# Moving the angles, magnitudes and folds that prepare batch 1 inside tile 0 of a Fourier-mixing and SwiGLU kernel

## The chip, the cores and the metric

The kernel runs on one core of one Trainium2 chip. The metric is the device time of one execution in microseconds (us), lower is better. Before the change it was 700.46 us, the median of three runs (700.24 to 701.84). The record marks a run as slow when it is over 1.5% above the fastest of its kernel.

## The reference

```python
def _attn_ref(x):                         # x: 8 x 3008 x 256, float32
    X = np.fft.fft(x, axis=1)
    X = np.fft.fft(X, axis=2)
    return X.real.astype(np.float32)

def _moe_ref(x, w_gate, w_val, w_out):    # x: 24064 x 256, d_ff = 1536
    g = x @ w_gate
    silu = g * (1.0 / (1.0 + np.exp(-g)))
    val = x @ w_val
    return (silu * val @ w_out).astype(np.float32)

# reference: _moe_ref of _attn_ref(x), reshaped to 24064 x 256
```

## The kernel before

The kernel folds each batch of x by its symmetries, does the long Fourier transform as matmuls against tables of cosines and sines, puts the short transform into the SwiGLU weights, and then works through tiles of about 512 columns. A tile has 12 *units*, one for each 128 of the 1536 features. A unit has a first half (`part_a`: gate and value of output row k, their product into `hp`) and a second half (`part_b`: the mirrored row, into `hm`), and the second half is issued one unit later. From tile 2 on, about half of the units are *split*: there GpSimd and not VectorE makes the two products.

The code below is in the order in which it is issued; the engines run it in parallel, each in its own order.

```python
# tmp_ctx: memory of the start, given back before the tiles; its space is used again (sg, hp, ...)
mm_, mM = col("mm", 4), col("mM", 4)      # small columns in tmp_ctx; mM = m / M
...
def angles(rr, kf, ch, t1):               # VectorE; reads mM
    for i in range(2):
        vstt(rr[:, i, :], kf, mM[:, 2 * ch + i:2 * ch + i + 1], t1[:, i, :],
             op0=Alu.mult, op1=Alu.subtract)

def magnitude(ra, rr):                    # VectorE: clears the sign bit
    vts(ra.bitcast(I32), rr.bitcast(I32), scalar1=0x7FFFFFFF, scalar2=None, op0=Alu.bitwise_and)

def sine(ch, lo, hi, rr):                 # ScalarE
    nc.scalar.activation(Tab[:, ch, :, 1, lo:hi], rr, AF.Sin, scale=sc, bias=zero)

def cosine(ch, lo, hi, ra):               # ScalarE, of the magnitude
    nc.scalar.activation(Tab[:, ch, :, 0, lo:hi], ra, AF.Sin, scale=-sc, bias=halfpi)
...
transform(0, 0, (1,), acc)                # end of the start
value_rows((0,))
for ch in range(2):
    angles(rrO[:, ch], kfO, ch, rrO[:, ch].bitcast(I32))
tmp_ctx.close()
...
# folds of batch b: kind "C" reads XC, kind "A" reads XA; all write SDf, on GpSimd
spread(("C", 1), 14, 1, 12)               # 14 steps over units 1 to 12
spread(("A", 1), 14, 13, 24)
...
def cosines(ch):
    magnitude(rrO[:, ch], rrO[:, ch])     # in place: the sine must have read it
    cosine(ch, NOO, NTAB, rrO[:, ch])

before = {1: weight_unit(1, 0), 2: weight_unit(1, 1),      # ahead of unit i
          3: [lambda: sine(0, NOO, NTAB, rrO[:, 0])],
          4: weight_unit(2, 0),
          5: [lambda: sine(1, NOO, NTAB, rrO[:, 1])],
          6: weight_unit(2, 1) + [lambda: cosines(0)],
          7: [lambda: cosines(1)],
          8: [lambda: weigh(NOO, NTAB)],
          9: [lambda: value_rows((1, 2))]}
...
for i, u in enumerate(units):
    for fn in before.pop(i, ()): fn()
    if i == 10:
        loads[0:0] = ((("A", 1), fn) for fn in load_a(1, nc.sync))   # x of batch 1
    run_loads(3)                          # three waiting loads a unit
    part_a(u)
    ...                                   # part_b of the unit before, output matmuls
    for what, j in fold_at.get(i, ()):
        fold_step(what, j, i)             # step 0 first issues all loads that it needs
```

The tables of 4i+1 (the cosines and sines of output rows 1, 5, 9 and so on) are needed by the second transform of batch 0, at the end of unit 9.

Of the kernel before, what the change touches and what calls it, by code (L numbers as in the profile page):

```python
# [12 lines left out]
F32 = mybir.dt.float32  # L13
I32 = mybir.dt.int32
# [17 lines left out]
def kernel(  # L32
# [11 lines left out]
    P = 128  # L44
    H = M // 2
    G = M // 8
# [15 lines left out]
    NOO = NCE + GH + 1  # L62
    NTAB = NOO + G
# [10 lines left out]
    const = ctx.enter_context(tc.tile_pool(name="const", bufs=1))  # L74
# [17 lines left out]
    CD = const.tile([P, 2, P], BF16, name="CD")  # L92
    SDt = const.tile([P, 2, P], BF16, name="SDt")
    m2 = const.tile([P, 1], F32, name="m2")
    wC = const.tile([P, 1], F32, name="wC")
    sgn = const.tile([P, 1], F32, name="sgn")
    XA = const.tile([P, 8, 2, D], F32, name="XA")
    XC = const.tile([P, 8, 2, D], F32, name="XC")
    SDf = const.tile([P, 2, 4, D], F32, name="SDf")
# [6 lines left out]
    rrO = XA.rearrange("p a q d -> p (a q d)")[:, 4 * T:4 * T + 4 * G].rearrange("p (c q n) -> p c q n", c=2, q=2)  # L106
    kfO = XA.rearrange("p a q d -> p (a q d)")[:, 4 * T + 4 * G:4 * T + 5 * G]
# [109 lines left out]
    q = nc.sync  # L217
# [48 lines left out]
    def col(name, n=1, dt=F32):  # L266
        small[name] = tp.tile([P, n], dt, name=name)
        return small[name]


    mm_, mM = col("mm", 4), col("mM", 4)

    def m_cols(ch, p, L, j0):
        h = col(f"h{ch}", 1, I32)
# [28 lines left out]
    def angles(rr, kf, ch, t1):  # L303
# [4 lines that stand above are left out]
    def magnitude(ra, rr):  # L308
        vts(ra.bitcast(I32), rr.bitcast(I32), scalar1=0x7FFFFFFF, scalar2=None, op0=Alu.bitwise_and)

    def sine(ch, lo, hi, rr):
        nc.scalar.activation(Tab[:, ch, :, 1, lo:hi], rr, AF.Sin, scale=sc, bias=zero)

    def cosine(ch, lo, hi, ra):
        nc.scalar.activation(Tab[:, ch, :, 0, lo:hi], ra, AF.Sin, scale=-sc, bias=halfpi)

    def weigh(lo, hi):
        vts(Tab[:, 1, 1, :, lo:hi], Tab[:, 1, 1, :, lo:hi], scalar1=wC, scalar2=None, op0=Alu.mult)
# [123 lines left out]
    def value_rows(fcs):  # L442

        n = T // P
        ps = psO.tile([P, T], F32, name="o")
        for fc in fcs:
            src = W0[1] if fc == 0 else Wraw[1][:, :, (fc - 1) * T:fc * T]
            for f in range(n):
                for no in range(2):
                    nc.tensor.matmul(ps[:, fc * n + f:fc * n + f + 1], src[:, no, f * P:(f + 1) * P],  # L450
                                     SDt[:, no, 0:1], start=(no == 0), stop=(no == 1))
        nc.scalar.copy(w0[:, fcs[0] * n:(fcs[-1] + 1) * n], ps[:, fcs[0] * n:(fcs[-1] + 1) * n])
# [154 lines left out]
    unfolded(1, 1, SBc, False, True)  # L607
    transform(0, 0, (1,), acc)
    value_rows((0,))
    for ch in range(2):  # L610
        angles(rrO[:, ch], kfO, ch, rrO[:, ch].bitcast(I32))

    tmp_ctx.close()

# [156 lines left out]
    def spread(what, n, lo, hi):  # L771
        seq.extend((lo + (i * (hi - lo)) // (n - 1), what, i) for i in range(n))

    spread(("C", 1), 14, 1, 12)
    spread(("A", 1), 14, 13, 24)
    lo = 25
    for b in range(2, B, 2):
        u = slot[(b, 0)] - 1
# [48 lines left out]
    def weights(fc, gv, k):  # L827
        transform_w(fc, gv, k, psO.tile([P, T], F32, name="o"))()

    def cosines(ch):  # L830
        magnitude(rrO[:, ch], rrO[:, ch])
        cosine(ch, NOO, NTAB, rrO[:, ch])

    def weight_unit(fc, gv):
        return [lambda k=k: weights(fc, gv, k) for k in range(2)]

    before = {1: weight_unit(1, 0), 2: weight_unit(1, 1),
              3: [lambda: sine(0, NOO, NTAB, rrO[:, 0])],
              4: weight_unit(2, 0),
              5: [lambda: sine(1, NOO, NTAB, rrO[:, 1])],  # L840
              6: weight_unit(2, 1) + [lambda: cosines(0)],
              7: [lambda: cosines(1)],
              8: [lambda: weigh(NOO, NTAB)],
              9: [lambda: value_rows((1, 2))]}
    loads = []

    prev = None
# [67 lines left out]
```

## Time and profile before

| what | before |
|---|---|
| median of the runs | 700.46 us |
| TensorE busy, share of the span | 97% |
| unit 0's first matmul, unit 10's first matmul | 25.87 us, 57.21 us |
| mean granted clock, 25 to 58 us | 0.79 |
| first matmul of unit 33's transform | 111.01 us |

First come three lines of the profile's page. The first gives each engine's busy time, share of the span and instructions; the others cut the span into 40 slices of 17.5 us, with busy tenths for PE (TensorE) and the clock that TensorE was granted, in tenths.

```profile
PE 679.1 (97%) x4369; PEld 415.5 (59%) x4369; DVE 519.6 (74%) x925; ACT 433.9 (62%) x765; POOL 593.8 (85%) x577
...
PE   7879989999999999999999999999999999999997
...
PEclk9979999999999999999999999999999999999999
```

After the seventh slice TensorE is as good as full and its clock is whole. Time can only be won before that. Of the slices after the start, the third (35 to 52 us) has a busy digit of 7 and a clock digit of 7, and the sixth (about 87 to 105 us) a busy digit of 8.

Next are lines of TensorE's timeline in tile 0. The columns are start and duration in us, engine, source line, operation, output and input; the brackets give the idle time before the instruction and what ended it.

```profile
30.90 0.36 PE L754 MATMUL g<-Qt,Wm 128*128 128x480 bf16 x1 [1.68 <-ACT sg L744]
31.59 0.36 PE L754 MATMUL v<-Qt,Wm 128*128 128x480 bf16 x1 [0.33 <-DVE hp L745]
...
42.24 0.37 PE L717 MATMUL g<-Pt,Wp 128*128 128x480 bf16 x1
42.44 0.37 PE L717 MATMUL g<-Qt,Wq 128*128 128x480 bf16 x1
...
42.85 0.37 PE L717 MATMUL v<-Qt,Wq 128*128 128x480 bf16 x1
46.16 0.56 PE L754 MATMUL g<-Qt,Wm 128*128 128x480 bf16 x1 [2.95 <-ACT sg L744]
...
47.20 0.61 PE L717 MATMUL g<-Pt,Wp 128*128 128x480 bf16 x1
47.60 0.61 PE L717 MATMUL g<-Qt,Wq 128*128 128x480 bf16 x1
```

There are two idle times. TensorE waits 1.68 us and then 0.33 us in unit 1 (at 30.90 and 31.59), and 2.95 us in unit 7. After the second one, matmuls of 480 columns start 0.40 us apart (47.20, 47.60), where before it they started 0.20 us apart (42.24, 42.44). The clock record has TensorE at half clock from 31.9 to 35.3 us and from 45.5 to 55.7 us.

The causes stand in the timelines of VectorE (DVE), ScalarE (ACT) and GpSimd (POOL).

```profile
27.12 3.00 DVE L305 SCALAR_TENSOR_TENSOR XA<-XA,mM 128x376 f32<-128x376 f32 x4
30.88 0.66 DVE L745 TENSOR_TENSOR hp<-sg,v 128x480 bf16<-128x480 f32 x1 [0.76 <-ACT sg L744]
...
42.56 2.14 DVE L309 TENSOR_SCALAR XA<-XA 128x752 int32<-128x752 int32 x1
...
47.28 0.75 DVE L309 TENSOR_SCALAR XA<-XA 128x752 int32<-128x752 int32 x1
```

```profile
30.28 0.57 ACT L744 ACTIVATE sg<-g 128x480 f32<-128x480 f32 x1 [4.07 <-DMA XC<-in_x_dram]
...
44.73 0.92 ACT L315 ACTIVATE Tab<-XA,halfpi 128x752 bf16<-128x752 f32 x1 [2.92 <-DVE XA L309]
```

```profile
39.62 4.67 POOL L152 TENSOR_TENSOR SDf<-XC 64x1024 f32<-64x1024 f32 x2
...
46.93 0.69 POOL L437 TENSOR_SCALAR Wm<-Wq,m_89 128x512 bf16<-128x512 bf16 x1
...
50.40 0.69 POOL L437 TENSOR_SCALAR Wm<-Wq,m_89 128x512 bf16<-128x512 bf16 x1
...
69.78 4.67 POOL L152 TENSOR_TENSOR SDf<-XA 128x1024 f32<-128x1024 f32 x2 [6.13 <-DMA XC<-in_x_dram]
...
90.10 1.28 POOL L737 TENSOR_TENSOR hp<-sgv,vv 128x512 bf16<-128x512 f32 x1
...
95.39 2.35 POOL L152 TENSOR_TENSOR SDf<-XC 128x1024 f32<-128x1024 f32 x1 [1.32 <-DMA XA<-in_x_dram]
```

The four angle operations fill VectorE from 27.12 to 30.12, and the first Silu of unit 0 (`sg`, ScalarE) starts at 30.28 although its input was ready near 27. The profile names a load as what ended the 4.07 us of idle; the semaphores that this instruction waits for in the built program include VectorE's last angle operation, because `sg` lies in the memory that the start's small columns give back. In unit 7 the first cosine waits 2.92 us for a magnitude that took 2.14 us, while GpSimd was in its two 64x1024 folds (39.62 to 44.29).

GpSimd's first value product (`hp`) runs at 90.10, among the last steps of batch 1's second folds, which began at 69.78 after 6.13 us of waiting for x.

### The profile page before, as it was taken

To read this page: it belongs to the slowest core of one execution; us is meant where nothing else is said; L and a number is where in the kernel's file an instruction comes from. 1 tells how busy PE (TensorE), PEld (TensorE's weight loads), DVE (VectorE), ACT (ScalarE), POOL (GpSimd) and SP (SyncE) were. 2 spreads that over 40 slices of the span, in tenths; PEclk is the share of its full clock that TensorE was granted. 3 is DMA by queue.
4 is the path that set the end of the run, shared out by engine and by line. 5 is a ranking of instruction groups with operands and counts; after the bars stand their busy time and mean duration, and the time that the engine had idled before them with its cause. 6 is when DMAs were issued, how large, how long until landed. Compare 5 with 4: busy or idle time off the path is not lost.

```text
span 698.6 us, 13274 instructions
## 1 busy us (share of the span) xinstructions
PE 679.1 (97%) x4369; PEld 415.5 (59%) x4369; DVE 519.6 (74%) x925; ACT 433.9 (62%) x765; POOL 593.8 (85%) x577
## 2 busy tenths in 40 slices
PE   7879989999999999999999999999999999999997
PEld 4335655566565566565665656655666556656676
DVE  8776667777777778677777777777777777788862
ACT  7465655566565666565665666656666566656663
POOL 7896999899999999999998989998899655658930
PEclk9979999999999999999999999999999999999999
DMA  9636353241612412316125111117111011111112
GB/s 216 112 46 132 107 136 93 63 121 44 160 32 65 132 46 71 111 46 160 34 65 138 39 34 43 46 38 152 37 47 46 31 31 46 45 31 46 46 46 69
DMA packets 45567, 52.55 MB, mean 75 GB/s; under 512 B 6290, under 2 KB 33466, under 8 KB 45498
## 3 DMA queue, kind: packets, MB, share of 16 engines
q1 hardware_dynamic: 42314, 49.35, 26.0%
q0 software_dynamic: 3184, 2.36, 2.5%
q8 instruction: 34, 0.56, 0.3%
q14 instruction: 35, 0.29, 0.1%
HBM read 29.39 MB, written 24.65 MB: 77 GB/s over the span
## 4 chain that ended last, share of the span: by engine, by line
PE 83%; DMA 4%; DVE 4%; issue 4%; POOL 2%; ACT 1%; SPq 1%; ACTq 0%; POOLq 0%; DVEq 0%
PE o L677 32%; PE v L717 16%; PE g L717 15%; PE g L754 8%; PE v L754 4%; PE g L566 3%; PE v L566 3%; DVE vv L736 2%; DMA XC<-in_x_dram 2%; DMA XC_107<-in_x_dram 1%; DMA XA<-in_x_dram 1%; POOL hm L759 1%; DVE vv L734 1%; POOL hp L737 1%; PE g L854 1%
## 5 line engine op out<-in xcount | busy, mean ns | idle before, releaser
L737 POOL TENSOR_TENSOR hp<-sgv,vv 128x512 bf16<-128x512 f32 (+1 forms) x132 | 168.2, 1276 | 49.9 <-DVE vv L734 39.0
L759 POOL TENSOR_TENSOR hm<-sgv,vv 128x512 bf16<-128x512 f32 (+1 forms) x132 | 167.7, 1275 | 8.5 <-ACT sgv L758 8.1
L677 PE MATMUL o<-Wo,hm 128*128 128x256 bf16 (+2 forms) x1140 | 170.5, 273 | 0.0
L677 PE MATMUL o<-Wo,hp 128*128 128x256 bf16 (+2 forms) x1140 | 169.6, 273 | 0.0
L677 PEld LDWEIGHTS <-hp 128*128 128x128 bf16 (+2 forms) x1140 | 111.9, 98 | 68.1 <-issue 8.2
L677 PEld LDWEIGHTS <-hm 128*128 128x128 bf16 (+2 forms) x1140 | 112.2, 99 | 65.8 <-issue 6.6
L732 DVE SCALAR_TENSOR_TENSOR es<-bc,w_85,v 128x512 f32<-128x512 f32 (+1 forms) x132 | 98.1, 743 | 53.0 <-PE v L717 52.8
L745 DVE TENSOR_TENSOR hp<-sg,v 128x512 bf16<-128x512 f32 (+2 forms) x156 | 103.7, 665 | 36.7 <-ACT sg L744 35.9
L744 ACT ACTIVATE sg<-g 128x512 f32<-128x512 f32 (+2 forms) x156 | 90.8, 582 | 45.9 <-PE g L717 41.0
L762 ACT ACTIVATE sg<-g 128x512 f32<-128x512 f32 (+2 forms) x156 | 91.1, 584 | 44.4 <-PE g L754 44.2
L763 DVE TENSOR_TENSOR hm<-sg,v 128x512 bf16<-128x512 f32 (+2 forms) x156 | 103.2, 661 | 19.0 <-ACT sg L762 8.9
L754 PE MATMUL g<-Qt,Wm 128*128 128x512 bf16 (+2 forms) x288 | 108.8, 378 | 5.2 <-ACT sg L744 5.1
L717 PE MATMUL v<-Pt,Wp 128*128 128x512 bf16 (+2 forms) x288 | 108.6, 377 | 2.4 <-DVE vv L736 2.4
L758 ACT ACTIVATE sgv<-g 128x512 f32<-128x512 f32 (+1 forms) x132 | 78.9, 598 | 50.1 <-PE g L754 41.3
L717 PE MATMUL g<-Qt,Wq 128*128 128x512 bf16 (+2 forms) x288 | 108.6, 377 | 0.5 <-DVE Qt L579 0.5
L717 PE MATMUL g<-Pt,Wp 128*128 128x512 bf16 (+2 forms) x288 | 108.8, 378 | 0.1
L729 ACT ACTIVATE sgv<-g 128x512 f32<-128x512 f32 (+1 forms) x132 | 78.7, 596 | 45.0 <-PE g L717 35.9
L734 DVE SCALAR_TENSOR_TENSOR vv<-v,es 128x512 f32<-128x512 f32 (+1 forms) x132 | 91.1, 690 | 19.7 <-POOL hp L737 1.7
L736 DVE SCALAR_TENSOR_TENSOR vv<-v,es 128x512 f32<-128x512 f32 (+1 forms) x132 | 89.7, 680 | 6.2 <-POOL hm L759 3.3
L717 PEld LDWEIGHTS <-Wp 128*128 128x128 bf16 x576 | 56.6, 98 | 42.1 <-issue 5.8
L152 POOL TENSOR_TENSOR SDf<-XA 128x1024 f32<-128x1024 f32 x28 | 66.1, 2365 | 8.0 <-DMA XC<-in_x_dram 6.1
L683 ACT COPY ev<-o 128x512 f32<-128x512 f32 x90 | 52.8, 587 | 30.6 <-PE o L677 29.6
(173 smaller groups left out, 742.2 us busy)
## 6 DMA issues: line engine op xcount, KB each, us to landing
out_dram<-ev SPq DMA_DIRECT2D x96, 128.0 KB
XA<-in_x_dram SPq DMA_DIRECT2D x32, 256.0 KB
XA<-in_x_dram SPq DMA_DIRECT2D x112, 64.0 KB
XC<-in_x_dram SPq DMA_DIRECT2D x105, 32.0 KB
XC<-in_x_dram SPq DMA_DIRECT2D x28, 120.0 KB
out_dram<-ev SPq DMA_DIRECT2D x12, 120.0 KB
out_dram<-ev SPq DMA_DIRECT2D x10, 112.0 KB
XA<-in_x_dram SPq DMA_DIRECT2D x1, 1024.0 KB
```

What stands on the lines that cost most here:

```text
L677: nc.tensor.matmul(ps[:n, j, :], hts[minus][:, f, c:c + n], Wo[:, f, :], start=(f == 0), stop=(f == nF - 1))
L717: nc.tensor.matmul(ps[:, :w], Wt[:, gv, fs], src[:, :w], start=start, stop=stop, skip_group_check=True)
L732: stt(es[:, :w], bc[t][:, :w], w0[:, f:f + 1], e[:, :w], op0=Alu.mult, op1=Alu.add)
L734: stt(vp[:, :w], o[:, :w], -0.5, es[:, :w], op0=Alu.mult, op1=Alu.add)
L736: stt(vm[:, w - 1::-1], o[:, :w], 0.5, es[:, :w], op0=Alu.mult, op1=Alu.add)
L737: nc.gpsimd.tensor_tensor(hts[t][0][:, f, :w], sg[:, :w], vp[:, :w], op=Alu.mult)
L744: nc.scalar.activation(sg[:, :w], g[:, :w], AF.Silu)
L745: nc.vector.tensor_tensor(hts[t][0][:, f, :w], sg[:, :w], v[:, :w], op=Alu.mult)
L754: nc.tensor.matmul(ps[:, :w], Wm[:, gv, f * P:(f + 1) * P], Qt[:, :w], start=False, stop=True, skip_group_check=True)
L759: nc.gpsimd.tensor_tensor(hts[t][1][:, f, :w], sg[:, :w], v[:, :w], op=Alu.mult)
L762: nc.scalar.activation(sg[:, :w], g[:, :w], AF.Silu)
L763: nc.vector.tensor_tensor(hts[t][1][:, f, w - 1::-1], sg[:, :w], v[:, :w], op=Alu.mult)
```

## The change

The intent is to take the table work of 4i+1 out of TensorE's way: no angles ahead of the first Silu, no sine that must come before an in-place magnitude, and magnitudes done before GpSimd starts its folds. The magnitudes now go to memory of their own. That memory is SDf, so the folds, which also write SDf, start at unit 6.

```diff
+    mM = const.tile([P, 4], F32, name="mM")          # kept for good
-    mm_, mM = col("mm", 4), col("mM", 4)
+    mm_ = col("mm", 4)
 ...
     value_rows((0,))
-    for ch in range(2):
-        angles(rrO[:, ch], kfO, ch, rrO[:, ch].bitcast(I32))
     tmp_ctx.close()
 ...
-    spread(("C", 1), 14, 1, 12)
-    spread(("A", 1), 14, 13, 24)
+    spread(("C", 1), 14, 6, 14)
+    spread(("A", 1), 14, 15, 24)
 ...
-    before = {1: weight_unit(1, 0), 2: weight_unit(1, 1),
-              3: [lambda: sine(0, NOO, NTAB, rrO[:, 0])],
-              4: weight_unit(2, 0),
-              5: [lambda: sine(1, NOO, NTAB, rrO[:, 1])],
-              6: weight_unit(2, 1) + [lambda: cosines(0)],
-              7: [lambda: cosines(1)],
-              8: [lambda: weigh(NOO, NTAB)],
-              9: [lambda: value_rows((1, 2))]}
+    raO = SDf...[:, 0:4 * G]                         # cut: viewed as channel, half, column
+    def angles_o(ch):
+        return [lambda: angles(rrO[:, ch], kfO, ch, rrO[:, ch].bitcast(I32)),
+                lambda: magnitude(raO[:, ch], rrO[:, ch])]
+    def cosine_o(ch):
+        return [lambda: cosine(ch, NOO, NTAB, raO[:, ch])]
+    def sine_o(ch):
+        return [lambda: sine(ch, NOO, NTAB, rrO[:, ch])]
+    before = {0: angles_o(0), 1: weight_unit(1, 0), 2: weight_unit(1, 1), 3: angles_o(1) + cosine_o(0),
+              4: weight_unit(2, 0) + cosine_o(1), 5: weight_unit(2, 1), 7: sine_o(0), 8: sine_o(1),
+              9: [lambda: weigh(NOO, NTAB), lambda: value_rows((1, 2))]}
```

More of the change, by code (lines that the diff above doesn't have):

```diff
@@ L828, in weights @@
         transform_w(fc, gv, k, psO.tile([P, T], F32, name="o"))()
-    def cosines(ch):
-        magnitude(rrO[:, ch], rrO[:, ch])
-        cosine(ch, NOO, NTAB, rrO[:, ch])
     def weight_unit(fc, gv):
         return [lambda k=k: weights(fc, gv, k) for k in range(2)]
-    before = {1: weight_unit(1, 0), 2: weight_unit(1, 1),
-              3: [lambda: sine(0, NOO, NTAB, rrO[:, 0])],
-              4: weight_unit(2, 0),
-              5: [lambda: sine(1, NOO, NTAB, rrO[:, 1])],
-              6: weight_unit(2, 1) + [lambda: cosines(0)],
-              7: [lambda: cosines(1)],
-              8: [lambda: weigh(NOO, NTAB)],
-              9: [lambda: value_rows((1, 2))]}
+    raO = SDf.rearrange("p k a d -> p (k a d)")[:, 0:4 * G].rearrange("p (c q n) -> p c q n", c=2, q=2)
+    def angles_o(ch):
[8 more added lines that the diff above has]
+              9: [lambda: weigh(NOO, NTAB), lambda: value_rows((1, 2))]}
     loads = []
```

## The prediction

> **What bounds it.** TensorE is 97% busy over the span and 99% from 110 us on (busy time by stretch), so only the start can give. Two places there lose TensorE time.
>
> 1. Tile 0 (26 to 57 us). The timeline shows TensorE idle 1.68 us before 30.90 (the first Silu starts at 30.28, after the four angle operations on VectorE, 27.12 to 30.12) and 2.95 us before 46.16. The second: ScalarE's cosine waits 2.9 us for a VectorE magnitude that took 2.14 us where its twin at 47.28 took 0.75; GpSimd was in a 64x1024 fold. The Trainium skill, "SBUF — State Buffer", calls their shared ports an exclusive lock; 2.14 against 0.75 agrees. After both idles the granted clock is 0.50, 31.8 to 35.2 and 45.5 to 55.7 us: a 480-column matmul steps every 0.40 us instead of 0.20. The skill, "TensorE: Matmul & The Clock Gate", Part 1, gives a 3.4 us activity window; the lengths are one and three of them.
>
> 2. 100 to 107 us. GpSimd is still in batch 1's second folds when its value products are due; TensorE waits 2.39 us for a VectorE value operation that waited for GpSimd, then runs at half clock 103.5 to 106.9.
>
> **What changes.** The built order moves nothing outside the first ~30 units. The first Silu's tile reused memory of the m/M column, so it waited for the last angle (the built program's semaphore wait names it). Now it waits only for work done at 17 us and should start near 27.2. VectorE does ch 0's angles (2 x 0.75) and magnitude (0.75, plus up to ~1.5 waiting for GpSimd) before the first product: that product goes from 30.88 to about 29.5 to 31.5, little gain. Unit 3 gets the same, about 1.2 us of delay. Cosines and sines no longer wait. So the 2.95 us idle, the 0.48 us one and most of the half-clock stretch (about 4.5 us of loss) go. Estimate for the end of tile 0: 5 to 7 us earlier, VectorE (about 20 us of work) the new limit.
>
> **How much survives.** GpSimd's batch-1 first folds run 39.6 to 63.6 in before, behind its backlog, so unit 6 costs nothing. Its next folds waited 6.13 us for x, landing at 69.78. The loads now start 5 us earlier, but the new order issues the last two behind tile 0's first three output stores (68.37 before, about 62.5 now): 62.5 + 1.7 + 1.3 + about 2.5 to land = 68 (estimate). GpSimd gains about 2 us there, and about 1.3 more where batch 2's load held it (95.39). TensorE, 6 us ahead, meets GpSimd in tile 2 and waits longer than before, perhaps one more half-clock window. I expect about 3 us of the 6 to remain.
>
> **Prediction: 697.4 us, 80% range 694.0 to 700.2. Faster by over 2%: 0.02; within 2%: 0.97; slower by over 2%: 0.01.**
>
> **What would show each step.** First Silu near 27.2 us. No wait of a cosine for VectorE; both magnitudes before 41 us. Clock 1.0 from about 36 to 90 us, with tile 0 ending near 51. GpSimd's batch-1 second folds starting near 67 to 68 us. TensorE idle at 90 to 104 grown from 2.6 to about 5 us. After 110 us a constant shift.
>
> **What would make it wrong.** If the magnitudes sit long behind GpSimd, TensorE falls to half clock again and tile 0 gains only 2 to 3 us: net nothing. If the last two loads land sooner, or GpSimd isn't what TensorE waits for at 90 to 104, up to 6 us survive.

## More of the kernel before

`weight_unit(2, 0)` and `weight_unit(2, 1)` each end with a GpSimd operation that scales a block of `Wm` (128 x 512, bf16). The second halves of units 8 to 11 read these blocks.

In the GpSimd lines the scalings of the last `Wm` blocks (`L437`, 46.93 and 50.40) stand behind folds.

## The result

| | before | after |
|---|---|---|
| median, same chip, four runs each | 700.44 us (700.24 to 701.84) | 694.33 us (693.12 to 694.45) |
| ratio, 95% interval | | 0.9905 (0.9888 to 0.9922) |
| profiled run: span | 698.6 us | 691.4 us |
| unit 0's first matmul | 25.87 us | 24.93 us |
| unit 0 to unit 3 | 9.79 us | 6.62 us |
| unit 3 to unit 7 | 6.58 us | 8.43 us |
| unit 7 to unit 10 | 14.97 us | 7.68 us |
| unit 0 to unit 10 | 31.34 us | 22.73 us |
| unit 10 to unit 33's transform | 53.80 us | 56.12 us |
| unit 33's transform to the end | 587.6 us | 587.6 us |

Ratios here and below are the mean time of one kernel's fast runs over that of the other's of the same rounds, so not quite the ratio of the quoted medians. The middle rows are times from one unit's first matmul to another's, read from TensorE's timeline; the last one is the span less the transform's start.

The change is faster by 0.95%. Its median lies at the lower end of the predicted range (694.0 to 700.2), and the gain of 6.1 us is twice the 3.0 us forecast. In the profiles tile 0 gains 8.61 us, the stretch up to unit 33 loses 2.32 us of it, and from there on the two kernels take the same time. The 0.94 us by which unit 0 began earlier belongs to this pair of profiles and not to the change: in eleven further profiles unit 0 began anywhere from 24.94 to 26.62 us, and before's 25.87 lies among them.

The same three lines of the page after the change (slices of 17.3 us):

```profile
PE 673.5 (97%) x4369; PEld 414.4 (60%) x4369; DVE 517.9 (75%) x925; ACT 433.4 (63%) x765; POOL 593.4 (86%) x577
...
PE   7999979999999999999999999999999999999997
...
PEclk9999999999999999999999999999999999999999
```

The third slice's clock digit went from 7 to 9. The sixth slice (about 86 to 104 us) stays below full: its busy digit fell from 8 to 7. TensorE's timeline in tile 0 after the change:

```profile
29.28 0.36 PE L753 MATMUL v<-Qt,Wm 128*128 128x480 bf16 x1 [0.79 <-DVE hp L744]
...
35.95 0.36 PE L753 MATMUL v<-Qt,Wm 128*128 128x480 bf16 x1 [0.80 <-DVE hp L744]
...
37.12 0.59 PE L430 MATMUL o<-XA,SDt 128*128 128x512 bf16 x2 [0.37 <-DVE Wp L440]
...
40.58 0.37 PE L716 MATMUL v<-Qt,Wq 128*128 128x480 bf16 x1
40.78 0.37 PE L753 MATMUL g<-Qt,Wm 128*128 128x480 bf16 x1
```

The idle in unit 1 is 0.79 us where it was 2.01. Unit 3's added VectorE work shows as 0.80 us at 35.95 and 0.37 us at 37.12. In unit 7 (from 39.98) TensorE goes from 40.58 to 40.78 without a wait where it had idled 2.95 us, and matmuls keep their step of 0.20 us. Waits of 0.18 to 0.20 us remain in units 3 and 8 and behind unit 9.

The timelines of VectorE, ScalarE and GpSimd that answer to those shown of before:

```profile
26.18 1.12 DVE L306 SCALAR_TENSOR_TENSOR XA<-XA,mM 128x376 f32<-128x376 f32 x2
27.34 1.32 DVE L310 TENSOR_SCALAR SDf<-XA 128x752 int32<-128x752 int32 x1
28.58 0.64 DVE L744 TENSOR_TENSOR hp<-sg,v 128x480 bf16<-128x480 f32 x1
...
34.62 0.72 DVE L310 TENSOR_SCALAR SDf<-XA 128x752 int32<-128x752 int32 x1
```

```profile
26.37 0.57 ACT L743 ACTIVATE sg<-g 128x480 f32<-128x480 f32 x1 [1.10 <-DMA XC<-in_x_dram]
...
32.51 0.94 ACT L316 ACTIVATE Tab<-SDf,halfpi 128x752 bf16<-128x752 f32 x1
...
35.37 0.92 ACT L316 ACTIVATE Tab<-SDf,halfpi 128x752 bf16<-128x752 f32 x1 [0.53 <-DVE SDf L310]
```

```profile
39.17 1.36 POOL L438 TENSOR_SCALAR Wm<-Wq,m_89 128x512 bf16<-128x512 bf16 x2
40.61 4.67 POOL L153 TENSOR_TENSOR SDf<-XC 64x1024 f32<-64x1024 f32 x2
...
65.14 4.67 POOL L153 TENSOR_TENSOR SDf<-XA 128x1024 f32<-128x1024 f32 x2 [2.60 <-DMA XC<-in_x_dram]
...
85.44 1.26 POOL L736 TENSOR_TENSOR hp<-sgv,vv 128x512 bf16<-128x512 f32 x1
...
89.66 2.35 POOL L153 TENSOR_TENSOR SDf<-XC 128x1024 f32<-128x1024 f32 x1 [0.28 <-DMA XA<-in_x_dram]
```

The first Silu now starts at 26.37, 1.44 us after unit 0's first matmul (4.41 us before). The magnitudes took 1.32 and 0.72 us, at 27.34 and 34.62, long before TensorE needs the tables; only channel 1's cosine, issued right behind its magnitude, waited, 0.53 us. GpSimd does both `Wm` scalings at 39.17, ahead of the folds. And these are the waits of TensorE in tile 2, after the change:

```profile
87.39 0.38 PE L716 MATMUL g<-Pt,Wp 128*128 128x512 bf16 x1 [0.90 <-ACT sgv L757]
...
90.16 0.57 PE L716 MATMUL v<-Qt,Wm 128*128 128x512 bf16 x1 [1.97 <-DVE vv L735]
...
97.55 0.38 PE L716 MATMUL v<-Pt,Wp 128*128 128x512 bf16 x1 [1.64 <-DVE vv L735]
```

TensorE idles 0.90, 1.97 and 1.64 us here, and 0.22 us more at 98.14: 4.73 us in all, where before it idled 2.39 and 0.22 us, 2.61 in all. The longest chain behind them is TensorE from VectorE's value operation, which waits for a buffer that GpSimd's product frees. GpSimd's first product is at 85.44, 4.66 us earlier than before, while TensorE had come 9.55 us earlier to unit 10.

### The profile page after: what moved, and what is told of

The parts are those of the page before. It is cut to its first block, busy times and chain, and to the rows that moved or that the text cites. A ratio compares the mean times of both kernels' runs of the same rounds, so it can differ in the third digit from the quotient of the medians.

```text
span 691.4 us, 13273 instructions
## 1 busy us (share of the span) xinstructions
PE 673.5 (97%) x4369; PEld 414.4 (60%) x4369; DVE 517.9 (75%) x925; ACT 433.4 (63%) x765; POOL 593.4 (86%) x577
## 4 chain that ended last, share of the span: by engine, by line
PE 85%; DMA 4%; DVE 4%; issue 3%; POOL 1%; SPq 1%; ACT 1%; ACTq 0%; POOLq 0%; DVEq 0%
PE o L676 33%; PE v L716 17%; PE g L716 15%; PE g L753 8%; PE v L753 4%; PE g L567 3%; PE v L567 3%; DVE vv L735 2%; DMA XC<-in_x_dram 2%; DMA XC_108<-in_x_dram 1%; SPq L139 1%; DMA XA<-in_x_dram 1%; DVE vv L733 1%; DMA out_dram<-ev 1%; PE g L856 1%
```

## The experiments

All kernels gave correct results. Each diff is against the kernel that is named. "Unit 0 to 10" is the time from unit 0's first to unit 10's first matmul in the run's profile.

| run | median us | ratio to before, 95% interval | unit 0 to 10 | unit 0 to transform 33 |
|---|---|---|---|---|
| (before, profile of the first section) | 700.44 | | 31.34 | 85.14 |
| (after, profile of the last section) | 694.33 | 0.9905 (0.9888, 0.9922) | 22.73 | 78.85 |
| e1_angles_only | 698.90 | 0.9976 (0.9947, 1.0006) | 29.14 | 84.72 |
| e2_order_only | 695.15 | 0.9920 (0.9891, 0.9949) | 23.65 | 79.64 |
| e3_one_port | 701.26 | 1.0017 (0.9982, 1.0053) | 28.30 | 82.96 |
| e4_folds_back | 698.18 | 0.9961 (0.9933, 0.9989) | 28.68 | 82.73 |
| after_again | 693.29 | 0.9895 (0.9870, 0.9919) | 22.73 | 78.69 |
| e5_loads_first | 695.19 | 0.9917 (0.9891, 0.9942) | 22.74 | 79.99 |
| e6_four_loads | 693.89 | 0.9897 (0.9870, 0.9924) | 22.73 | 78.48 |
| e7_two_on_vector | 691.33 | 0.9865 (0.9836, 0.9893) | 22.73 | 75.47 |
| e8_both | 689.98 | 0.9841 (0.9813, 0.9869) | 22.77 | 73.79 |
| e9_three_on_vector | 688.49 | 0.9820 (0.9793, 0.9848) | 22.75 | 72.46 |
| e10_folds_only | 702.14 | 1.0015 (0.9991, 1.0039) | 29.76 | 85.38 |

Before itself spread far more than its first runs had shown: eleven runs on one chip took 697.32 to 704.27 us. On that chip the longer ones tended to the lower mean clock (correlation -0.79); on the two other chips, eleven runs each, the correlation was -0.65 and +0.22, so the clock is not shown to be the whole reason. The changed kernel's six runs, on the second chip, took 693.22 to 694.84 us, where before took 697.71 to 702.94. So a single profile of a kernel with the old stalls tells how long a stall was, but not what it costs on average.

Why it does not can be read from the profiles. The clock changes only at the borders of windows of 3.41 us. With the busy time added up between these borders, the thirteen profiles show this from unit 0 on: after each of the 15 full-clock windows in which TensorE was busy for 0.81 to 1.57 us came half clock, and it came after none of the windows with 1.68 us or more; one window of 1.54 us, in e6, went without. So it took about 1.6 us of work in a window to keep the clock, and a stall that falls across a border can go free. Half clock went on after the 8 windows with 2.80 us or less of busy time and ended after the 15 with 3.08 or more.

### e1_angles_only: the start alone

```diff
# against before
+    mM kept in a tile of its own; angles at the end of the start taken out
+    before = {0: angle_o(0), ...,
+              3: [lambda: sine(0, NOO, NTAB, rrO[:, 0])] + angle_o(1), ...}   # angles alone
```

> Before with only two parts of the change: the m/M column kept, and the angles of channel 0 at unit 0, of channel 1 at unit 3. Sines first, in-place magnitudes at units 6 and 7 and the folds stay as before. Theory (three independent gains: start of tile 0 about 3.2 us less about 1 us that unit 3 gives back, the cosine stall at unit 7 about 7.3 us, then a loss of 2 to 3 us to GpSimd in tile 2): first Silu 4 us earlier relative to unit 0's first matmul, first product on VectorE about 1.5 to 2.3 us earlier, no half clock in units 1 and 2; the stall of about 3 us at unit 7 and three half-clock windows stay. Unit 0 to unit 10 on TensorE about 29 us (31.3 before, 22.7 after); total 698.5 to 700, 0.5 to 2 us faster than before. Rival (the start stall sets everything, the cosine stall follows from a phase of the clock): unit 0 to 10 near 24 us, total near 695.

Unit 0 to 3 fell to 5.88 us (9.79 in before) with no half clock there; the idle of unit 7 stayed, 2.93 us, with three half-clock windows behind it. Unit 0 to 10 took 29.14 us. The total is at best a little lower: the interval holds 1. The start's stall is a gain of its own in tile 0, but it is the small part of the change, and the rival falls.

### e2_order_only: the rest alone

```diff
# against after
-    mM in a tile of its own; angles in angles_o
+    mM back in the start's memory; angles of both channels at the end of the start
+    # magnitudes still at units 0 and 3, cosines first, folds from unit 6
```

> The changed kernel with the angles of both channels back at the end of the start and the m/M column back in its temporary memory; magnitudes at units 0 and 3, cosines before sines, folds from unit 6 as in the change. Theory: the start loses as in before (first Silu about 4.4 us after unit 0's first matmul, TensorE idle about 2 us, one half-clock window), the unit 7 stall and its three half-clock windows are gone. Unit 0 to unit 10 on TensorE about 24 to 25 us; total 694.5 to 697, that is 4 to 6 us faster than before. Rival (start stall decides): unit 0 to 10 near 30, total near 699.

Unit 0 to 10 took 23.65 us and the total is 0.8% below before. The stall of unit 1 was there in full (1.68 and 0.83 us), yet in this profile the clock stayed whole through tile 0, so that it cost less than in before's profile: a window border divided it, and TensorE was busy for 2.20 and 2.07 us of the two windows, where before's one window had 1.41. This part of the change carries most of the gain. The two parts together are worth about 0.95 to 1.05%, the parts 0.8 and 0.24%.

### e3_one_port: an attempt to take the magnitudes off the shared port

```diff
# against before, in cosines(ch)
-        magnitude(rrO[:, ch], rrO[:, ch])
+        by2 = rrO[:, ch].rearrange("p q (n two) -> p q two n", two=2)
+        magnitude(by2, by2)
```

> Before, with the two in-place magnitudes at units 6 and 7 taken through a stride of two elements (same values, the same place in every queue). Theory of the shared ports: in before the first magnitude's 2.14 us were 1.73 us of waiting for GpSimd's fold (it ended 0.41 us after that fold). A strided form should not wait: both take 0.8 us or so each, whatever GpSimd runs. The first cosine then starts 1.3 us earlier and TensorE's idle at unit 7 falls from 2.95 to about 1.6 us; with so little idle the clock may stay up. If it does, unit 0 to 10 falls from 31.3 to 25 to 26 us and the total to 695.5 to 697.5; if it drops for one window or more, 698 to 700. Rival (the place in VectorE's queue alone makes the stall, not the ports): the first magnitude still takes about 2 us and the total stays within 0.5 us of before.

The experiment did not do what it was made for. Its two magnitudes, in VectorE's timeline:

```profile
40.47 1.08 DVE L309 TENSOR_SCALAR XA<-XA 128x752 int32<-128x752 int32 x1
...
44.13 1.08 DVE L309 TENSOR_SCALAR XA<-XA 128x752 int32<-128x752 int32 x1
```

Both took 1.08 us, and in the trace each ended 0.41 us after the end of the GpSimd instruction that was running when it was due (a fold step that ended at 41.14, and one that ended at 44.80). The GpSimd work behind each became longer by about 0.3 us (the two fold steps together 4.97 us for 4.67, a copy 0.51 for 0.19). So the strided form took the ports too: it waited for GpSimd and then ran for the same 0.41 us. That is also how long after GpSimd's instruction the others ended: 0.41 us in before's 2.14 us magnitude and 0.40 in its 0.75 us one, 0.41 in the changed kernel's first. The durations of 2.14, 0.75 and 1.08 us differ by where in GpSimd's instruction VectorE arrived. The Trainium skill, "VectorE: DVE Perf Modes", section "What auto-detection actually checks", lists for the mode that puts both ports on one source (2×_2P) a single source, source and destination in SBUF, and the outermost dimensions, and no stride; that agrees with this run. Its magnitudes only met GpSimd at another point, so that TensorE idled 1.74 and 1.80 us where before had 2.95 and 0.48. In its profile, the fastest of its six runs, one window at half clock followed instead of three, and unit 0 to 10 took 28.30 us; the total over the six is that of before. Whether the stall without any port wait would be short enough is left open by this run; e10 below bears on it.

### e4_folds_back: the folds where before has them

```diff
# against after; the magnitudes get 3 KB of their own, so that SDf is free for folds
+    raO = const.tile([P, 2, G], F32, name="raO")
-    spread(("C", 1), 14, 6, 14)
-    spread(("A", 1), 14, 15, 24)
+    spread(("C", 1), 14, 1, 12)
+    spread(("A", 1), 14, 13, 24)
-    3: angles_o(1) + cosine_o(0)
+    3: cosine_o(0) + angles_o(1)         # one tile for both channels
```

> The changed kernel with the magnitudes in 3 KB of their own (channel 0's cosine issued ahead of channel 1's magnitude) so that the folds can stand where before has them: batch 1's first folds from unit 1, second ones from unit 13. My prediction held that starting the folds at unit 6 costs nothing; it didn't see that GpSimd also scales the last weight block (Wm of unit 4's and 5's transforms) and that in before these two stand behind folds. Theory: TensorE reaches unit 8's Wm matmul at about 44 us and the second scaling ends near 50 us, so TensorE idles about 5 us and the clock drops; unit 0 to 10 about 28 to 31 us, total 697 to 700. Rival (the fold placement is only a matter of memory): unit 0 to 10 near 22.7 us as in the change; with all of batch 1's loads ahead of the first stores again, total 692.5 to 694.5.

TensorE's waits in tile 0, and the GpSimd lines that ended them:

```profile
48.04 0.58 PE L754 MATMUL g<-Qt,Wm 128*128 128x480 bf16 x1 [3.07 <-POOL Wm L439]
50.01 0.58 PE L754 MATMUL v<-Qt,Wm 128*128 128x480 bf16 x1 [1.40 <-POOL Wm L439]
```

```profile
40.14 4.68 POOL L154 TENSOR_TENSOR SDf<-XC 64x1024 f32<-64x1024 f32 x2
...
47.29 0.69 POOL L439 TENSOR_SCALAR Wm<-Wq,m 128x512 bf16<-128x512 bf16 x1
...
49.26 0.69 POOL L439 TENSOR_SCALAR Wm<-Wq,m 128x512 bf16<-128x512 bf16 x1
```

Through unit 9 this kernel is as fast as the changed one (18.23 us from unit 0 to unit 9 in both). Then TensorE waits 3.07 and 1.40 us for the `Wm` scalings that stand behind the folds, drops to half clock, and takes 28.68 us to unit 10. The later folds thus do not only make room for the magnitudes: they put the last weights ahead of 10 us of fold work. Two thirds of the gain of tile 0 (5.95 of 8.61 us) hang on that.

### e10_folds_only: the folds alone

```diff
# against before
-    spread(("C", 1), 14, 1, 12)
-    spread(("A", 1), 14, 13, 24)
+    spread(("C", 1), 14, 6, 14)
+    spread(("A", 1), 14, 15, 24)
```

> Before, with nothing but the folds moved: batch 1's first folds from unit 6 to 14, second ones from 15 to 24. Theory (moving the folds is needed only once TensorE no longer stalls at unit 7; it frees the last weight block's scaling from behind them): the Wm scalings end near 43 instead of 51 us, but TensorE still stalls at unit 7 on the in-place magnitudes, so ratio to before 0.997 to 1.003. Rival (the folds' place is a gain by itself): ratio below 0.996.

The total is that of before, as the theory had it. The profile shows why, in VectorE's magnitudes and in TensorE's waits:

```profile
42.04 0.60 DVE L309 TENSOR_SCALAR XA<-XA 128x752 int32<-128x752 int32 x1
...
45.22 2.33 DVE L309 TENSOR_SCALAR XA<-XA 128x752 int32<-128x752 int32 x1
```

```profile
44.10 0.36 PE L754 MATMUL g<-Qt,Wm 128*128 128x480 bf16 x1 [1.25 <-ACT sg L744]
...
49.02 0.56 PE L754 MATMUL g<-Qt,Wm 128*128 128x480 bf16 x1 [3.05 <-ACT sg L744]
```

GpSimd was held by the weight scalings for longer, its folds began at 42.31 instead of 39.62, and so the first magnitude met only a scaling and took 0.60 us. The second met a fold and took 2.33 us. TensorE's two waits turned around with them: 1.25 us after the short magnitude, 3.05 us after the long one, where before had 2.95 us after its 2.14 us and 0.48 us after its 0.75 us, the latter already at half clock. This splits the stall, as far as two units of one run can: even with next to no port wait, a cosine that must follow an in-place magnitude on another engine left TensorE 1.25 us idle; behind the magnitude that took 1.73 us longer the idle was 1.8 us longer.

### after_again, e5_loads_first, e6_four_loads: what holds GpSimd in tile 1

```diff
# against after
-        run_loads(3)
+        run_loads(4 if 10 <= i < 15 else 3)     # e5
+        run_loads(4)                            # e6
```

> The changed kernel once more, beside the next three on one chip, since before itself spread from 697.3 to 704.3 us on the chip of the first four experiments. All theories: 693 to 695 us, ratio to before 0.988 to 0.993.

> The changed kernel with four loads of x a unit in units 10 to 14, so that all of batch 1's loads go ahead of tile 0's first stores; nothing else changes. My prediction held that the two loads behind the stores hold GpSimd and so bound what survives. In the changed kernel GpSimd waited 2.60 us for them (65.14). Theory (GpSimd's backlog bounds the gain): the second folds start when the first ones end, near 62.5, 2.6 us earlier; then batch 2's first load, which GpSimd met with 0.28 us of waiting, is the next limit, so only about 0.5 to 1.5 us reach the total: 693 to 694 where the change has 694.3. Rival (TensorE's loss in tile 2 has another cause): same total as the change within 0.3 us although the folds start 2.6 us earlier.

> The changed kernel with four loads of x a unit throughout instead of three. Theory: GpSimd's second folds of batch 1 start near 62.5 as in the run before, and batch 2's loads land early enough that GpSimd runs on without a gap: first fold of batch 2 near 87 (89.66 in the change), TensorE's idle at 80 to 100 falls from 4.7 to about 2.5 us, total about 2 us below the change, 691.5 to 693. Rival: stores held back behind loads take it back, total equal to the change.

The repeat of the changed kernel gave 693.29 us, so its gain stands. The theory of e5 fell at its first step: with the last two loads issued by 57.0 instead of 60.7 us (61.0 in the repeat), ahead of the stores, GpSimd still began its second folds at 65.80 (65.55 in the repeat). In both, 22 us pass from the first load's issue to that fold. Issuing the two loads ahead of the stores did not make them land sooner. The total, 695.19, is even 1.9 us above the repeat's; why is not shown, but in its profile the half clock of tile 2 lasted two windows and not one. e6 had 65.75 too and the changed kernel's total, 693.89. GpSimd went from product to fold without a gap at 89.95, but so it did in the repeat at 89.77, so that the larger supply of loads shows no gain there. TensorE idled 5.9 us in tile 2 all the same, in pieces, without falling to half clock in the profiled run. Loads alone are not what binds there.

### e7_two_on_vector, e8_both, e9_three_on_vector: GpSimd's products

```diff
# against after; split() for units of tile 2
+        if u in ((2, 0), (2, 2)):               # e7 and e8; e9 adds (2, 3)
+            return False
-        if f == 0 and split((t, SPLIT[0])):
+        if f == 0 and split((t, 5)):
# e8 and e9 also have run_loads(4)
```

> The changed kernel with the first two split units of tile 2 (features 0 and 2) done unsplit, so that VectorE and not GpSimd makes their four products; two more matmuls of 0.216 us. Theory: GpSimd is the only thing TensorE waits for at 80 to 100 us; without four products of 1.27 us there it is 5.1 us less behind, TensorE's 4.7 us of idle shrink to under 1 us, no half-clock window there, total 3 to 5 us below the change: 689.5 to 691.5. Rival (the wait follows batch 2's loads, which land at 89.5 whatever the products do): idle only moves, total within 1 us of the change.

> The changed kernel with both of the last two edits: features 0 and 2 of tile 2 unsplit, and four loads of x a unit. With the first alone GpSimd stood 2.33 us waiting for batch 2's load at 89.21 and TensorE idled 3.0 us after it; with the second alone the load was there but GpSimd's backlog reached to 89.95. Theory (backlog and load are each enough to hold GpSimd at 89 to 90 us): together the first fold of batch 2 starts near 87, TensorE's idle at 80 to 102 falls to about 1 us, total 689 to 690.5, about 1.5 us below the run with the first alone. Rival (one of the two is not a limit): within 0.5 us of 691.3.

> As the run before, with feature 3 of tile 2 unsplit too. Theory: GpSimd has slack there now, so two products less move nothing but one more matmul of 0.216 us comes in: within 0.7 us of the run before, either side. If it is more than 1 us faster, GpSimd's products were still what TensorE waited for.

With two units fewer on GpSimd the time fell by 2 us on the same chip. TensorE's idle in tile 2 fell from 4.6 us in the repeat to 3.0 us, and GpSimd, done with batch 1 at 86.88, now waited for x of batch 2:

```profile
86.68 0.20 POOL L172 TENSOR_TENSOR BBa<-SDf 128x2 bf16<-128x2 f32 x1
89.21 4.67 POOL L153 TENSOR_TENSOR SDf<-XC 128x1024 f32<-128x1024 f32 x2 [2.33 <-DMA XC<-in_x_dram]
```

That is less than the theory expected, and for the reason that its rival named: a second limit stood right behind the first. With both edits (e8) TensorE idled 1.46 us and the median was 689.98 us, as expected; but batch 2's first fold began at 89.21 and not near 87, after 1.64 us of waiting (unit 0 began 1.7 us later in this profile than in e7's). The third unit (e9) was expected to change nothing and gave another 1.5 us: no wait of TensorE from 74 to 106 us is left in its profile, and the clock stays whole from unit 0 to the end. By the rule set ahead of the run, GpSimd's products were still what TensorE waited for in e8. At 688.49 us, e9 beats both kernels (0.9820 of before). The changed kernel's repeat and e9 ran on different chips, so the ratios to before, 0.9895 and 0.9820, are to be compared.

## Why the prediction was right or wrong

**Where the time is won: right.** Only tile 0 gained, tile 2 gave part of it back, and from unit 33 on the shift is constant (587.6 us in both).

**The first Silu: right.** It was freed of the last angle and starts 1.44 us after unit 0's first matmul; the prediction's 27.2 us would have been 1.33.

**Unit 7: right in mechanism, about right in size.** The 2.95 us, the 0.48 us and the half clock are gone; unit 7 to 10 takes 7.29 us less, where 7.9 had been put down (2.95, 0.48 and 4.5).

**"Little gain" in the first units: wrong.** The prediction took the time of VectorE's first product (30.88 to 29.5 or later) for what unit 1 gains, and left the first half-clock window in place ("Clock 1.0 from about 36"). The product started at 28.58, or 3.65 us after unit 0's first matmul instead of 5.01. With the Silu out of the way, TensorE's idle there fell from 2.01 to 0.79 us, and the clock never dropped. Unit 0 to 3 took 3.17 us less; e1, which moves the angles but no magnitude, shows 3.91 us. Against that, unit 3 cost 1.85 us where 1.2 had been estimated. The sum 3.17 - 1.85 + 7.29 gives 8.61 us for the tile, and the prediction worked with 6. So the step that failed is the cost of the start's stall: about nothing was put down for it, and it measured 3.17 us, the only one of the three terms that came out better than predicted. About half of it belongs to the half-clock window of before's profile: e3 and e10 have the same start without one, and took 8.17 and 8.16 us from unit 0 to 3, against 9.79 in before and 6.62 after the change.

**What survives: wrong in size, and in one reason.** Of 8.61 us, 6.29 remained, a loss of 2.32 where 3 had been predicted. That the forecast came this near is partly luck, since one of its reasons failed. TensorE's idle in tile 2 grew from 2.61 to 4.73 us as forecast (about 5), and e7 to e9 show that GpSimd's backlog, together with batch 2's loads, is its cause. But GpSimd's second folds began at 65.14 and not at 68: the first stores were issued at 58.30 and not near 62.5, as TensorE was 9.55 us ahead and not 6. And the reason given for 68, that the last two loads stand behind the stores, was not borne out by e5. From the first load's issue to the fold, 2 MB took 21.81 us in the changed kernel and 18.60 to 22.94 over the thirteen profiles. In the first ten of these us (44 to 54) the DMA engines were busy for 0.53 of the time and moved 90 GB/s (0.52 and 76 GB/s in e5). Why they keep to this pace is left open.

**"Unit 6 costs nothing": right, but it missed the point.** The folds' new place is what lets the `Wm` scalings arrive in time; e4 without it loses 5.95 us of the tile's gain. The prediction did not mention these scalings at all.

**The ports: right, but 0.75 us was the wrong base.** The long magnitude was a wait for GpSimd. It was no free duration either: every magnitude of this size measured ran for about 0.4 to 0.5 us after the GpSimd instruction that it had met.

The Trainium skill, "TensorE: Matmul & The Clock Gate", Part 1, was used for the window of about 3.4 us; the lengths of half clock in these runs (3.41, 6.83 and 10.24 us) agree with it. The prediction did not carry it through: a busy window at half clock does about 1.7 us less work (3.41 us at 0.40 us a matmul instead of 0.20), so that removing the 2.01 us of idle in unit 1 also removed the window behind it, in before's profile at least; where in a window the same stall falls decides that.

## What to carry to other kernels

An operation that feeds a table long in advance should be placed where no engine waits for it, and an in-place step that ties two readers of the same data across engines (here sine, magnitude, cosine) makes such a wait, as e10 shows. The change took it away by a second buffer and an earlier place together; no run here tells the two apart. When a stall near the length of the clock's window is removed, count its idle and the half-clock time behind it together, count small stalls too, and take more than one profile, since the stall's place in the window decides whether half clock follows. When one engine gains a lead, look at once for the next engine in line, here GpSimd with folds, weight scalings and products in one queue: the order inside that queue decided how much of the lead remained.

## What the Trainium skill lacked or had wrong

- "TensorE: Matmul & The Clock Gate": its advice is to avoid idle gaps of more than about 3 us. Here shorter ones brought half clock: 1.68 and 0.33 us close together in before's profile, and 2.39 us in its tile 2. Others of the like did not: 1.68 and 0.83 us in e2, 2.38 us in e6. The page does not say what share of a window must be idle; in the thirteen profiles half clock followed 15 windows with at most 1.57 of 3.41 us busy, and none with 1.68 or more. What it says of the window's free-running phase fits.
- The same page gives one busy window as what ends the half clock, and not how busy it must be. Here windows with 2.80 us or less of busy time did not end it and windows with 3.08 or more did: in before it lasted three windows, 45.5 to 55.7 us, of which the first two had 2.62 and 2.80.
- "SBUF — State Buffer" says that the later of the two engines blocks for the whole instruction. The runs agree and give the price: with 752 elements of 32 bits a magnitude ended 0.40 to 0.52 us after the GpSimd instruction it met, so that its duration ran from 0.60 to 2.33 us in e10 alone.
- "GPSIMD Engine Reference" gives cycles per element. That a fold over 64 partitions takes as long as one over 128 (two of 1024 columns: 4.67 us in both) follows from its account of 16 partitions to each of GpSimd's eight cores, but no sentence warns of it.
